# A first room in plain fp32, the smallest room moved to last but one, and a last room that finishes its first tile ahead

## The chip, the cores and the metric

The kernel runs on one NeuronCore of a Trainium2 chip. The metric is the device time of one execution in microseconds (us); the version before was timed in three runs. TensorE (PE in the profile) does matrix products, with its weight loads shown apart as PEld; VectorE (DVE) and ScalarE (ACT) do elementwise work; GpSimd (POOL) prepares indirect transfers; SyncE (SP) issues the plain ones.

## The reference

Attention with a causal window of 128 positions over 8 batches of 576 positions, 8 heads of 64, and then a mixture of experts. A gate keeps the previous token's expert or takes the best one for this token, so a batch's routing is a sequential scan; then each token goes through one of 8 experts (512 to 1024 to 512, with a relu between), scaled by its gate probability.

```python
scores = np.where(mask, scale * q @ k.T + bias, -1e9)          # mask: 0 <= rel < 128
attn = exp(scores - max) / (sum + 1e-09);  x = attn @ v         # x: (8, 576, 512)
for b in range(B):
    for s in range(S):
        fresh_e = argmax(logits[b, s])
        e = fresh_e if s == 0 or local_gate[b, s] < 0.5 else prev_e
        h = np.maximum(x[b, s] @ w1[e], 0.0)
        out[b, s] = p[e] * (h @ w2[e])
```

## The kernel before

**Attention and routing.** The first part works through 32 slots (8 batches, 4 pairs of heads). A recording layer keeps the order of each engine there as it is written, so its instructions all carry the line of one helper, L167; the tables `ORDER` and `LAST` give that order. The tokens of a batch are written to a table in device memory (`xd`). A generator (`tokens`, then `route`) computes the batch's experts step by step between the attention work: PE, ACT and DVE take turns at small operations, each on the result of the one before. The routing of batch 7 can start only when attention is done. It is then advanced by `tick()` calls inside the first visits of the second part, and so are the tables that place the tokens.

**Visits.** The second part is a row of 15 visits (`PLAN`, `visits`, L1200). A visit takes up to 512 rows that one expert has to process, gathers them from `xd` (GpSimd, one indirect transfer for 128 blocks of 128 values, `take`), and multiplies them by that expert's weights. Three visits belong to experts 0, 1 and 2 (256, 384 and 512 rows, the first two known before batch 7 is routed). The other 12 are rooms for the experts by rank of what is left; `ORDER_OF_ROOMS` (L29) sets their order, and their experts are read from a register. In that order the rooms have 512, 288, 384, 416, 256, 288, 384, 192, 256, 384, 224 and 32 rows.

**One visit.** `Fixed.run` (L1021) goes over f = 0..7, eight slices of 128 of the hidden 1024. For each f, PE makes h (four steps kc, N columns), then ACT the relu hh and DVE the rest hl = relu(h) - hh; then `second(f - 1)` adds to one output tile y for each 128 rows. Every product is three matmuls (`three`, L1003 to L1006) of fp32r operands, high times high, high times low and low times high. So the weights and the rows are split in two beforehand. A weight chunk (two slices f of w1 or w2, 512 KB, `wraw`) is cast by ACT (L241) and subtracted by DVE (L243) into `cut`, of which there are six (`SPLITS`), each freed by the visit's last use of the chunk. `wraw` has six buffers too (`RAWS`). The gathered rows (`kr`) are split by `split_x`: per 128 rows a DVE transpose (L188), an ACT cast (L191) and a DVE subtraction (L192) into `qx`; the transposed rows have one buffer, `xtr`. `finish` scales a y by its gate values (ACT or DVE in turn), and `scatter` (L998) writes it to the output rows with an indirect transfer from GpSimd.

**The row of visits.** `Feed` gathers and splits the rows ahead. At each `tick` of a visit it does at most one split step (`turn`) for rows of the next visit and one gather, and every third tick one scatter. After a visit, `Feed.finish` does what is still missing for the next one. The last visit, `Mini` (32 rows), works in plain fp32 with unsplit weights: `first` (L1094) runs inside the visit before, ahead of its last `second`, `turn` transposes, and `Mini.run` (L1108, matmuls at L1084) has no ticks. Where the engines are not pinned to the program's order, the build's scheduler sets it.

## Time and profile before

| what | value |
|---|---|
| median of three runs | 679.7 us (679.34 to 679.98) |
| the profiled execution | 678.48 us, of which the span of the trace is 676.8 us |
| TensorE busy | 656.5 us, 97% of the span |
| DVE, ACT, POOL busy | 466.0, 418.1, 392.6 us |
| HBM traffic | 101.03 MB read, 19.29 MB written |

The profile lists instructions with a start, a duration, engine, line and tiles; an idle stretch ahead of one stands in brackets with what ended it. Durations of PE rows overlap, because matmuls are pipelined: the pace of a series is read from the starts, and a busy share near 100% may hide waits shorter than a matmul. A plain fp32 matmul has two PE rows, an fp32r one has one. In the listing of one visit the three kinds L1004, L1005 and L1006 are the three products of `three`. The execution's time is 1.7 us longer than the span of its trace.

### The profile page before, as it was taken

The page shows a single profiled execution, that of the slowest core. Times are in us where ns is not written, and L with a number is a line of the kernel's source. Part 1 is how long each engine was busy: PE and PEld are TensorE (multiplying, and loading weights), DVE is VectorE, ACT ScalarE, POOL GpSimd, SP SyncE. Part 2 cuts the span into 40 slices and gives each one's busy share as a digit, 9 for nine tenths or more (in the row PEclk, how much of TensorE's full clock was granted, in tenths as well). Part 3 has the DMA queues.
Part 4 walks back from the last instruction along what each step waited for, and adds up shares of the span by engine and source line. Part 5 has one row for each costly group of instructions (what it writes and reads, how often), then busy time and mean ns, then how long its engine had stood idle before and what let it go on. Part 6 is the DMA issues. An engine that isn't in the chain of part 4 may idle for free. (4 is left out here: it accounts for less than half of the span.)

```text
span 676.8 us, 16362 instructions
## 1 busy us (share of the span) xinstructions
PE 656.5 (97%) x5485; PEld 528.0 (78%) x5485; DVE 466.0 (69%) x1637; ACT 418.1 (62%) x1217; POOL 392.6 (58%) x655
## 2 busy tenths in 40 slices
PE   8999999999999989999999999999999999999993
PEld 4667777677666678878888888988898898899882
DVE  6579889889888999975553657453776547774520
ACT  7999999999989644343442555353665536653421
POOL 7856656556687745877775476471577516761011
PEclk9999999999999999999999999999999999999998
DMA  9855754764813675554654268343846834774810
GB/s 287 275 143 156 240 170 144 218 194 152 255 68 110 196 265 179 164 148 148 228 189 135 82 225 281 96 133 128 287 152 205 281 99 143 241 224 152 274 54 34
DMA packets 60903, 121.09 MB, mean 179 GB/s; under 512 B 9260, under 2 KB 28204, under 8 KB 60816
## 3 DMA queue, kind: packets, MB, share of 16 engines
q1 hardware_dynamic: 51248, 100.12, 46.5%
q0 software_dynamic: 9136, 19.30, 9.3%
q8 instruction: 44, 0.72, 0.4%
q10 hardware_dynamic: 432, 0.59, 0.3%
q14 instruction: 43, 0.35, 0.2%
HBM read 101.03 MB, written 19.29 MB: 178 GB/s over the span
## 5 line engine op out<-in xcount | busy, mean ns | idle before, releaser
L182 POOL DMA_INDIRECT kr<-xd,xidx x141 | 155.3, 1101 | 55.3 <-issue 39.4
L1004 PE MATMUL h<-qx,cut 128*128 128x384 f32 (+6 forms) x440 | 142.4, 324 | 0.0
L1005 PE MATMUL h<-qx,cut 128*128 128x384 f32 (+6 forms) x440 | 140.8, 320 | 0.2 <-DVE qx L192 0.2
L1006 PE MATMUL h<-qx,cut 128*128 128x384 f32 (+6 forms) x440 | 140.9, 320 | 0.0
L243 DVE TENSOR_TENSOR cut<-wraw,cut 128x512 fp32r<-128x512 f32 x183 | 118.8, 687 | 30.0 <-ACT cut L241 28.6
L1056 ACT ACTIVATE hh<-h 128x384 fp32r<-128x384 f32 (+4 forms) x104 | 46.6, 448 | 132.9 <-PE h L1006 131.2
L167 POOL TENSOR_SCALAR cut<-cut,r 128x192 f32<-128x192 f32 (+2 forms) x256 | 99.6, 407 | 45.8 <-DVE r L167 16.2
L998 POOL DMA_INDIRECT out<-y,sidx x41 | 44.5, 1085 | 132.7 <-ACT y L1013 85.3
L1057 DVE SCALAR_TENSOR_TENSOR hl<-h,hh 128x256 fp32r<-128x256 f32 (+4 forms) x112 | 55.4, 496 | 88.4 <-ACT hh L1056 88.0
L1004 PE MATMUL y<-cut,hh 128*128 128x512 f32 x288 | 113.7, 395 | 0.8 <-ACT hh L167 0.8
L1006 PE MATMUL y<-cut,hl 128*128 128x512 f32 x288 | 113.1, 394 | 0.9 <-DVE hl L1057 0.9
L1005 PE MATMUL y<-cut,hh 128*128 128x512 f32 x288 | 113.3, 393 | 0.0
L167 ACT ACTIVATE cut<-scs,mn 128x192 f32<-128x192 f32 (+2 forms) x256 | 108.8, 429 | 5.3 <-DVE mn L167 5.0
L241 ACT CAST cut<-wraw 128x512 fp32r<-128x512 f32 x164 | 93.6, 618 | 24.6 <-PE y L1006 23.9
L1004 PEld LDWEIGHTS h<-qx,cut 128*128 128x128 f32 x440 | 83.0, 189 | 9.7 <-issue 3.9
L167 DVE CUSTOM_DVE_ANT_0 scs<-sc,bias 128x192 f32<-128x192 f32 (+2 forms) x288 | 83.1, 324 | 8.9 <-PE sc L167 5.6
L1005 PEld LDWEIGHTS h<-qx,cut 128*128 128x128 f32 x440 | 83.1, 189 | 5.7 <-DVE qx L192 0.7
L1006 PEld LDWEIGHTS h<-qx,cut 128*128 128x128 f32 x440 | 83.2, 189 | 2.7 <-issue 0.2
L167 PE MATMUL pt<-ident,cut 128*128 128x128 f32 x448 | 70.8, 282 | 0.6
L1006 PEld LDWEIGHTS y<-cut,hl 128*128 128x128 f32 x288 | 54.0, 188 | 13.5 <-DVE hl L1057 2.1
L167 PE MATMUL sc<-kr,qx 64*64 64x192 f32 (+2 forms) x1152 | 61.9, 319 | 1.2 <-DVE mn L167 1.2
L1004 PEld LDWEIGHTS y<-cut,hh 128*128 128x128 f32 x288 | 54.2, 188 | 10.7 <-ACT hh L167 1.8
(218 smaller groups left out, 1036.7 us busy)
## 6 DMA issues: line engine op xcount, KB each, us to landing
wraw<-w SPq DMA_DIRECT2D x100, 512.0 KB
xT<-w SPq DMA_DIRECT2D x20, 512.0 KB
kr<-kT SPq DMA_DIRECT2D x31, 288.0 KB
qx<-qT SPq DMA_DIRECT2D x30, 288.0 KB
cut<-v SPq DMA_DIRECT2D x8, 1024.0 KB
xd<-T SPq DMA_DIRECT2D x8, 768.0 KB
xd<-T SPq DMA_DIRECT2D x8, 384.0 KB
kr<-xd,xidx POOLq DMA_INDIRECT x141, 3.8
```

Of the source, the lines that this page charges most:

```text
L167: ins = getattr(self.engine, name)(*args, **kw)
L182: queued(nc.gpsimd.indirect_dma_start(out=r, out_offset=None, in_=src[0:n, :], in_offset=bass.IndirectOffsetOnAxis(ap=col, axis=0), bounds ...
L241: scalar.copy(c[:, 0, f], raw[:, f])
L243: (pool if 2 * n + f == POOL_CUT else vector).tensor_tensor(c[:, 1, f], raw[:, f], c[:, 0, f], ALU.subtract)
L998: queued(nc.gpsimd.indirect_dma_start(out=out.rearrange("t (a c) -> (t a) c", a=n), out_offset=bass.IndirectOffsetOnAxis(ap=col, axis=0), ...
L1004: nc.tensor.matmul(o, ah, bh, start=start, stop=False)
L1005: nc.tensor.matmul(o, ah, bl, start=False, stop=False)
L1006: nc.tensor.matmul(o, al, bh, start=False, stop=stop)
L1056: now.act.activation(hh, hp[:, :M], AF.Relu)
L1057: nc.vector.scalar_tensor_tensor(hl, hp[:, :M], 0.0, hh, ALU.max, ALU.subtract)
```

## The change

Four things are altered.

- The first visit (expert 0, 256 rows) becomes `Plain`: its weights are marked "raw" and used as loaded, its rows are only transposed (`PlainRows`), h and y are plain fp32 matmuls, and there is one relu and no hl. The splitting of its first six chunks and rows is gone from the attention part (`turns`).
- `Stream` counts `wraw` buffers that are held (`live`) where it counted chunks ahead, and lets the splitting go on past chunks that are not split.
- `ORDER_OF_ROOMS` ends 192, 384, 224, 32, 256: the `Mini` room is last but one and the 256-row room of rank 2 is last.
- The last visit runs with `tail`: the scatters of earlier visits are issued ahead of it; the second products of its output tile 1 for f = 5, 6, 7 are kept back; after the last h, tile 0 is completed, finished and scattered, and then tile 1.

```diff
-ORDER_OF_ROOMS = [0, 1, 2, 8, 3, 9, 4, 10, 5, 6, 7, 11]
+ORDER_OF_ROOMS = [0, 1, 2, 8, 3, 9, 4, 10, 6, 7, 11, 5]
...
+    class PlainRows(Rows):
+        def turn(self, t):
+            if self.x is None:
+                self.x = sh.tile([P, self.blocks, KS, 32], F32, name="qx")
+            n = self.last(t)
+            pin(nc.vector.transpose(self.x[:, 4 * t:4 * t + n].rearrange("p b c i -> p (b c i)"), self.r[:, t, :n].rearrange("p q c -> p (q c)")))
...
-            while self.n_raw < len(self.order) and self.n_raw < self.n_cut + RAWS:
+            while self.n_raw < len(self.order) and self.live < RAWS:
...
-            while self.n_cut < len(self.order) and self.n_cut < self.first + self.depth:
+            while self.n_cut <= upto or self.n_cut < min(self.first + self.depth, self.ready):
                 self.load()
-                if self.order[self.n_cut][3] == "only":
+                if self.order[self.n_cut][3] in ("only", "raw"):
...
-        keep = "only" if nb == 1 else "also" if nb % 4 in (1, 2) else None
+        keep = "raw" if kind == "own" and e == 0 else "only" if nb == 1 else "also" if nb % 4 in (1, 2) else None
...
-            yield from W.split(tp.tile([P, 2, 2, DM], F32R, name="xT"), act, dve)
-            for what in (("M4", 4 * NB - 5), ("U3", 4 * NB - 2), ("M4", 4 * NB - 1)):
-                while what not in emitted:
-                    yield
-                yield from W.split(W.room(), act, dve)
...
-                if f > 0:
+                if tail and f == 6:
+                    vh, vl, _ = W.at("b")
+                    hh, hl = hs[5]
+                    three(ys[0], hh[:, 0:P], hl[:, 0:P], vh[:, 1], vl[:, 1], False, False)
+                elif f > 0 and not (tail and f == 7):
                     second(f - 1)
...
+            if tail:
+                assert n == 2 and not rest
+                chunks = [W.at("b"), W.at("b", 1)]
+                for t, fs in ((0, (6, 7)), (1, (5, 6, 7))):
+                    for f in fs:
+                        hh, hl = hs[f]
+                        sl, (vh, vl, _) = slice(P * t, P * t + P), chunks[f // 2 - 2]
+                        three(ys[t], hh[:, sl], hl[:, sl], vh[:, f % 2], vl[:, f % 2], False, f == 7)
+                    c = self.rows.t0 + t
+                    finish(ys[t], self.rows.g[:, t:t + 1], self.rows.idx[2][:, c:c + 1], t)
+                    scatter(*pending.pop())
...
+    class Plain(Fixed):
...
+            def second(f):
+                h, raw = hs.pop(f), W.at("b")
+                for t in range(n):
+                    nc.tensor.matmul(ys[t], h[:, P * t:P * t + P], raw[:, f % 2], start=f == 0, stop=f == 7)
+                    tick()
...
+            for f in range(8):
+                raw = W.at("a")
+                hp = ph_.tile([P, N], F32, name="h")
+                for kc in range(KS):
+                    nc.tensor.matmul(hp, raw[:, f % 2, P * kc:P * kc + P], self.rows.x[:, :, kc], start=kc == 0, stop=kc == KS - 1)
+                hs[f] = mp.tile([P, N], F32, name="hh", bufs=3)
+                now.act.activation(hs[f], hp, AF.Relu)
...
-            mini = visits[i + 1] if i + 2 == len(visits) else None
-            v.run(W, lambda: feed.tick(i + 1), mini, lambda: feed.finish(i + 1))
+            mini = visits[i + 1] if i + 1 < len(visits) and isinstance(visits[i + 1], Mini) else None
+            if i + 1 == len(visits):
+                while pending:
+                    scatter(*pending.pop(0))
+            v.run(W, lambda: feed.tick(i + 1), mini, lambda: feed.finish(i + 1), i + 1 == len(visits))
             feed.finish(i + 1)
```

Lines move by the edit: L1004 to L1006 become L1020 to L1022, L1084 becomes L1118, L241 and L243 become L248 and L250, L1013 becomes L1029, L1011 becomes L1027. L1171 and L1162 are the matmuls of `Plain` for h and y.

PE, where the routing of batch 7 begins inside the first visit (pk are the routing's small tiles). Before:

```order
L1006 MATMUL h_4945<-qx_4410,xT_4708 128x256
L1004 MATMUL y_4894<-cut_4842,hh_4928 128x512
L167 MATMUL pk_4936<-xT_4083,w32_98 32x128 x4
L1005 MATMUL y_4894<-cut_4842,hh_4928 128x512
L167 MATMUL pk_4966<-ident_81,part_4912 128x128 x4
L1006 MATMUL y_4894<-cut_4842,hl_4929 128x512
```

And now, where a row with x4 is four matmuls:

```order
L167 MATMUL pk_4879<-xT_4083,w32_98 32x512 x4
L1171 MATMUL h_4892<-qx_4410,wraw_4085 128x256
L1162 MATMUL y_4868<-wraw_4087,hh_4875 128x512
L167 MATMUL pk_4901<-xT_4083,w32_98 32x128 x4
L1162 MATMUL y_4869<-wraw_4087,hh_4875 128x512
L167 MATMUL pk_4916<-ident_81,part_4878 128x128 x4
L1171 MATMUL h_4928<-qx_4410,wraw_4089 128x256 x4
```

Between two routing steps stand whole plain matmuls now. Ahead of the 32x512 row stand 7 of the 32 h matmuls now, and 19 of the 96 before; behind it stand 25 h and all 16 y matmuls now, and 77 and 48 before.

ACT and then DVE at the end of the 224-row visit and the `Mini` room (hl_9553, hh_9561, y_9645 are the `Mini` room's, y_9580 and y_9582 the 224-row visit's, cut_9640 and qx_9647 the last visit's). Before, ACT ends with the `Mini` room:

```order
L1056 ACTIVATE hh_9940<-h_9927 128x224
L1099 ACTIVATE hl_9967<-h_9950 128x256
L1013 ACTIVATE y_9980<-y_9741,gs_9241 128x512
L1106 COPY hh_9975<-tr_9972 128x256
L1013 ACTIVATE y_10017<-y_9984,gs_9471 128x128
```

Now ACT has:

```order
L1133 ACTIVATE hl_9553<-h_9536 128x256
L1029 ACTIVATE y_9580<-y_9299,gs_8789 128x512
L1140 COPY hh_9561<-tr_9558 128x256
L248 CAST cut_9640<-wraw_9600 128x512 x2
L1029 ACTIVATE y_9645<-y_9584,gs_9021 128x128
L191 CAST qx_9647<-xtr_9648 128x4x128
L191 CAST qx_9647<-xtr_9652 128x4x128
L1072 ACTIVATE hh_9680<-h_9667 128x256
```

And DVE has:

```order
L1027 TENSOR_SCALAR y_9582<-y_9300,gs_8789 128x512
L250 TENSOR_TENSOR cut_9640<-wraw_9600,cut_9640 128x512 x2
L188 STREAM_TRANSPOSE xtr_9648<-kr_9310 128x512
L192 TENSOR_TENSOR qx_9647<-xtr_9648,qx_9647 128x4x128
L188 STREAM_TRANSPOSE xtr_9652<-kr_9310 128x512
L192 TENSOR_TENSOR qx_9647<-xtr_9652,qx_9647 128x4x128
```

The splitting of the last visit's rows stands behind the `Mini` room's work on both engines, after one chunk's splitting; five of its eight chunks are split further up.

PE behind the last h. Before, it ends with the second stage of the `Mini` room:

```order
L1004 MATMUL y_9742<-cut_9824,hh_9940 128x512
L1005 MATMUL y_9742<-cut_9824,hh_9940 128x512
L1006 MATMUL y_9742<-cut_9824,hl_9941 128x512
L1084 MATMUL y_9984<-wraw_9790,hh_9975 32x128 x8
L1084 MATMUL y_9984<-wraw_9829,hh_9975 32x128 x8
L1084 MATMUL y_9984<-wraw_9848,hh_9975 32x128 x8
L1084 MATMUL y_9984<-wraw_9879,hh_9975 32x128 x8
```

Now y_9665 is tile 0 of the last visit and y_9666 tile 1:

```order
L1020 MATMUL y_9665<-cut_9735,hh_9842 128x512
L1021 MATMUL y_9665<-cut_9735,hh_9842 128x512
L1022 MATMUL y_9665<-cut_9735,hl_9843 128x512
L1020 MATMUL y_9666<-cut_9640,hh_9799 128x512
L1021 MATMUL y_9666<-cut_9640,hh_9799 128x512
L1022 MATMUL y_9666<-cut_9640,hl_9800 128x512
L1020 MATMUL y_9666<-cut_9735,hh_9822 128x512
L1021 MATMUL y_9666<-cut_9735,hh_9822 128x512
L1022 MATMUL y_9666<-cut_9735,hl_9823 128x512
L1020 MATMUL y_9666<-cut_9735,hh_9842 128x512
L1021 MATMUL y_9666<-cut_9735,hh_9842 128x512
L1022 MATMUL y_9666<-cut_9735,hl_9843 128x512
```

Nine matmuls of tile 1 stand behind the last one of tile 0, and on GpSimd the two scatters of this visit are the only ones behind them.

## Rows read from the trace of the kernel before

**Rows 1.** Busy time by stretch of the span (us from its start): length, then for each engine busy us and instructions, the granted TensorE clock, DMA share and GB/s.

```profile
200.00:250.00 50.00, 47.38 (x448) 34.98 (x448) 46.59 (x179) 36.88 (x106) 34.62 (x54) 1.00 0.58 185
...
300.00:330.00 30.00, 30.00 (x134) 24.83 (x133) 15.40 (x24) 11.48 (x21) 22.69 (x22) 1.00 0.52 161
...
660.00:677.00 17.00, 5.18 (x100) 3.50 (x92) 0.75 (x1) 1.70 (x4) 2.94 (x3) 0.81 0.10 34
```

**Rows 2.** PE in order of time inside the first visit: start us, us, engine, line, operation. The first row is the routing's first step for batch 7; the last two L1006 rows end the visit and go on with the next one.

```profile
226.56 1.07 PE L167 MATMUL pk<-xT,w 128*32 128x512 f32 x8
...
231.27 0.50 PE L1006 MATMUL y<-cut,hl 128*128 128x512 f32 x1 [0.90 <-DVE hl L1057]
...
233.06 0.33 PE L167 MATMUL pk<-ident,part 128*128 128x128 f32 x1 [0.25 <-DVE L L167]
...
248.09 0.50 PE L1004 MATMUL y<-cut,hh 128*128 128x512 f32 x1 [0.78 <-ACT hh L167]
...
252.16 0.20 PE L167 MATMUL pk<-cw,ro_all 128*128 128x48 f16 x1 [0.62 <-DVE ro_all L167]
...
255.67 0.62 PE L1006 MATMUL y<-cut,hl 128*128 128x512 f32 x2
256.14 0.34 PE L1006 MATMUL h<-qx,cut 128*128 128x384 f32 x1
```

**Rows 3.** PE in order of time, two unbroken series of the first visit: six matmuls of 512 columns with the 256-column series behind them (first and last of each).

```profile
244.33 0.40 PE L1004 MATMUL y<-cut,hh 128*128 128x512 f32 x1
...
245.49 0.39 PE L1006 MATMUL y<-cut,hl 128*128 128x512 f32 x1
245.71 0.28 PE L1004 MATMUL h<-qx,cut 128*128 128x256 f32 x1
...
247.03 0.28 PE L1006 MATMUL h<-qx,cut 128*128 128x256 f32 x1
```

**Rows 4.** PE groups of plain fp32 matmuls, one line for each shape: count, busy us and mean ns. Four of them run beside each other, one in each quarter of the array's columns.

```profile
L167 PE MATMUL pk<-xT,w 128*32 128x512 f32 x8 | 1.1, 604 | 0.0
L1094 PE MATMUL h<-xT,qx 128*32 128x256 f32 x32 | 1.9, 382 | 0.0
```

**Rows 5.** DVE and ACT groups between 216 and 256 us: count, busy us and mean ns.

```profile
L243 DVE TENSOR_TENSOR cut<-wraw,cut 128x512 fp32r<-128x512 f32 x17 | 11.1, 687 | 0.1
...
L1057 DVE SCALAR_TENSOR_TENSOR hl<-h,hh 128x256 fp32r<-128x256 f32 x8 | 3.2, 414 | 0.0
...
L167 ACT CAST cut<-wraw 128x512 fp32r<-128x512 f32 x24 | 13.4, 622 | 0.3 <-PE y L1006 0.3
```

**Rows 6.** All engines at the end of attention, in order of time: a cast of the first visit's weights and one of its rows, a wait of PE for ACT, and between them a subtraction for the weights.

```profile
215.28 0.61 ACT L167 CAST xT<-wraw 128x512 fp32r<-128x512 f32 x1
215.79 0.61 ACT L191 CAST qx<-xtr 128x512 fp32r<-128x512 f32 x1
...
218.63 0.65 DVE L167 TENSOR_TENSOR xT<-wraw,xT 128x512 fp32r<-128x512 f32 x1
...
218.86 0.55 PE L167 MATMUL xb<-pt,cut 128*64 128x128 f32 x8 [0.66 <-ACT pt L167]
```

**Rows 7.** The splitting of 128 rows for a later visit, DVE and ACT in order of time (the third of four tiles of the 512-row visit).

```profile
286.27 0.71 DVE L188 STREAM_TRANSPOSE xtr<-kr 128x512 f32<-128x512 f32 x1
287.01 0.62 ACT L191 CAST qx<-xtr 128x512 fp32r<-128x512 f32 x1 [1.38 <-DVE xtr L188]
287.67 0.69 DVE L192 TENSOR_TENSOR qx<-xtr,qx 128x512 fp32r<-128x512 f32 x1
```

**Rows 8.** All engines but the weight loads at the end of the span, in order of time.

```profile
662.93 0.36 ACT L1106 COPY hh<-tr 128x256 f32<-128x256 f32 x1
663.26 0.75 DVE L1011 TENSOR_SCALAR y<-y,gs 128x512 f32<-128x512 f32 x1 [4.29 <-PE y L1006]
663.31 0.98 POOL L998 DMA_INDIRECT out<-y,sidx  x1 [14.54 <-ACT hh L1106]
663.35 1.96 PE L1084 MATMUL y<-wraw,hh 128*32 128x128 f32 x64
665.37 0.37 ACT L1013 ACTIVATE y<-y,gs 128x128 f32<-128x128 f32 x1 [2.08 <-PE y L1084]
667.23 0.98 POOL L998 DMA_INDIRECT out<-y,sidx  x1 [2.94 <-issue]
670.60 0.98 POOL L998 DMA_INDIRECT out<-y,sidx  x1 [2.39 <-issue]
```

**Rows 9.** The granted clock at the end of the span, in stretches as in the first group; and PE at its start, in order of time, eight and six warming matmuls of 512 columns.

```profile
669.00:670.00 1.00, 0.00 (x0) 0.00 (x0) 0.00 (x0) 0.00 (x0) 0.00 (x0) 1.00 0.28 105
670.00:671.00 1.00, 0.00 (x0) 0.00 (x0) 0.00 (x0) 0.00 (x0) 0.40 (x1) 0.69 0.00 0
...
1.06 3.59 PE L167 MATMUL pk<-warm 128*128 128x512 f16 x8 [1.06 <-DVE warm L167]
9.35 1.47 PE L167 MATMUL pk<-warm 128*128 128x512 f16 x6
```

**Rows 10.** What held up the scatters of L998 over the whole span (us, times), and the time from issue to landing of the weight chunks in `wraw` (us, min/median/max).

```profile
  DMA out<-y,sidx: 8.6, 3
...
DMA to landing us min/median/max: 2.8/3.1/6.5
```

**Rows 11.** The chain of work that ended last, its shares of the span by line.

```profile
by line: issue 0.3%; DMA out<-y,sidx 0.1%; POOL out L998 0.1%; POOLq L1294 0.1%
```

More of the change, by code (lines that the diff above doesn't have):

```diff
@@ L250, in __init__, with paired @@
             self.order = order
-            self.raw, self.cut, self.gone, self.n_raw, self.n_cut, self.first, self.depth = [], {}, set(), 0, 0, 0, 1
+            self.raw, self.cut, self.gone = [], {}, set()
+            self.n_raw = self.n_cut = self.n_room = self.first = self.live = self.ready = 0
+            self.depth = 1
+        def paired(self, i):
+            _, which, _, kind = self.order[i]
+            return kind in ("also", "only") and which == ("b" if kind == "also" else "a")
         def load(self):
-            while self.n_raw < len(self.order) and self.n_raw < self.n_cut + RAWS:
+            while self.n_raw < len(self.order) and self.live < RAWS:
                 e, which, c, kind = self.order[self.n_raw]
-                if kind and which == ("b" if kind == "also" else "a"):
+                if self.paired(self.n_raw):
+                    if self.n_raw > self.first + 2 * SPLITS:
+                        return
                     if c % 2 == 0:
@@ L281, in split, with find, at @@
             self.cut[self.n_cut] = c[:, 0], c[:, 1], raw
+            if not self.paired(self.n_cut):
+                self.live -= 1
             self.n_cut += 1
             yield from split_chunk(raw, c, scalar, vector, self.n_cut - 1 if self is W else 0)
-        def find(self, which):
-            return min(i for i in self.cut if self.order[i][1] == which)
-        def at(self, which):
+        def find(self, which, nth=0):
+            return [i for i in range(self.first, len(self.order)) if self.order[i][1] == which and i not in self.gone][nth]
+        def at(self, which, nth=0):
             self.depth = min(self.depth + 1, SPLITS)
-            self.fill()
-            return self.cut[self.find(which)]
+            i = self.find(which, nth)
+            self.fill(i)
+            return self.cut[i]
         def done(self, which):
@@ L296, in done @@
             self.gone.add(i)
+            if self.order[i][3] in ("only", "raw") and not self.paired(i):
+                self.live -= 1
             while self.first in self.gone:
@@ L803, in turns @@
                 yield
-            while not W.raw or NB - 2 not in read:
-                yield
-            yield from W.split(tp.tile([P, 2, 2, DM], F32R, name="xT"), act, dve)
-            for what in (("M4", 4 * NB - 5), ("U3", 4 * NB - 2), ("M4", 4 * NB - 1)):
-                while what not in emitted:
-                    yield
-                yield from W.split(W.room(), act, dve)
         known, taken, routed, read, emitted = [], [], [], [], []
-        rows0 = [Rows(4 * KS * e, KS * e, 4 * k, idx0, n) for e, (k, n) in enumerate(EARLY)]
+        rows0 = [(Rows if e else PlainRows)(4 * KS * e, KS * e, 4 * k, idx0, n) for e, (k, n) in enumerate(EARLY)]
         side, prep = iter(()), {":": setup(), ";": zeros()}
@@ L1019, in __init__, with run @@
             self.rows = rows
-        def run(self, W, tick, mini=None, ready=None):
+        def run(self, W, tick, mini=None, ready=None, tail=False):
             N = 32 * self.rows.blocks
@@ L1089, in first @@
         def first(self, W):
-            raws = [W.at("a") if i == 0 else W.cut[W.find("a") + i] for i in range(4)]
+            raws = [W.at("a", i) for i in range(4)]
             hp = ph_.tile([P, 256], F32, name="h")
@@ L1093, in first @@
                 for g in range(4):
-                    nc.tensor.matmul(hp[32 * g:32 * g + 32], self.rows.x[:, kc], raws[g][:, :, P * kc:P * kc + P], start=kc == 0, stop=kc == 3,
+                    nc.tensor.matmul(hp[32 * g:32 * g + 32], self.rows.x[:, 0, kc], raws[g][:, :, P * kc:P * kc + P], start=kc == 0, stop=kc == 3,
                                      skip_group_check=True)
@@ L1114, in run @@
             finish(y, self.rows.g[:, 0:1], self.rows.idx[2][:, c:c + 1], 0)
-    class MiniRows(Rows):
-        def turn(self, t):
-            self.x = sh.tile([P, KS, 32], F32, name="qx")
-            pin(nc.vector.transpose(self.x.rearrange("p c i -> p (c i)"), self.r[:, 0, 0]))
+    class Plain(Fixed):
+        def run(self, W, tick, *_):
+            N = 32 * self.rows.blocks
+            n = N // P
+            ys = [py.tile([P, DM], F32, name="y") for _ in range(n)]
+            hs = {}
+            def second(f):
[3 more added lines that the diff above has]
+                    tick()
+                if f % 2:
+                    W.done("b")
+            for f in range(8):
[5 more added lines that the diff above has]
+                now.act.activation(hs[f], hp, AF.Relu)
+                if f % 2:
+                    W.done("a")
+                tick()
+                if f > 0:
+                    second(f - 1)
+                tick()
+            second(7)
+            for t in range(n):
+                c = self.rows.t0 + t
+                finish(ys[t], self.rows.g[:, t:t + 1], self.rows.idx[2][:, c:c + 1], t % 2)
     class Flex:
```

15 lines of the change are left out of this document (10 added, 5 removed).

## Prediction

> **What bounds the kernel now.** I read the table of stretches first [rows 1]. From 300 us on TensorE is busy without a break while DVE and ACT are half idle: there only matmul work counts. Two places are different. In 200 to 250 us TensorE is short of 2.6 us while DVE runs 46.6 of 50: routing, splitting and rows compete there. And the last 17 us hold 5.2 us of TensorE. Then I read TensorE in order of time inside the first visit [rows 2]: its waits end on DVE or ACT operations. Last I read the end [rows 8]: the last matmul ends at 665.31, the last scatter starts at 670.60 and the span ends at 676.8. So the change can pay at the first visit and at the end, and nowhere else.
>
> **First visit, the matmuls.** A series of fp32r matmuls moves on by 0.12 us for 256 columns ((247.03 - 245.71) / 11) and 0.232 us for 512 ((245.49 - 244.33) / 5) [rows 3]. The visit has 96 of the first and 48 of the second: 11.5 + 11.1 = 22.6 us. In plain fp32 the 16 matmuls of L1094 have 32 rows, so eight steps with four side by side: (1.9 - 0.38) / 7 = 0.22 us a step [rows 4], two steps for one full matmul of 256 columns, 0.44 us. For 512 columns I take twice that, 0.88; the two steps of the 32x512 row, (1.07 - 0.60) = 0.47 apart [rows 2, 4], bound it at 0.94. So the visit needs 32 x 0.44 + 16 x 0.88 = 28.2 us: **5.6 us more** matmul work, on the engine that bounds.
>
> **First visit, the waits.** What pays for it are waits. From the routing's first step to the visit's end is 256.14 - 226.56, less two matmuls of the next visit in between (0.35): 29.2 us [rows 2]. In it stood 77 h and 48 y matmuls, 9.2 + 11.1 = 20.3 us. The other 8.9 us are the routing's own matmuls, whose first step takes 1.07 and which I put at 3.5 in all, and waits, 5.4. The four longest waits are 0.90, 0.25, 0.78 and 0.62 [rows 2], 2.55 together; the others are gaps that overlapping durations hide. Each ends with hl, hh or a routing step that stood in DVE's or ACT's queue behind splits. The change takes off those queues 16 of the split halves, 16 x 0.69 = 11 us on DVE and 16 x 0.62 = 10 us on ACT, and eight hl, 3.2 us [rows 5]; one half was given to GpSimd for a later visit and stays. Between two routing steps the order now has 0.9 to 7 us of plain matmuls, and DVE's steps fit under them. Two places stay tight: the scan waits for a hold that stands in ACT's queue behind a cast of the second visit, whose weights are loaded only when a plain chunk is freed and need 3.1 us to land [rows 10]; and ro_all has two chunks and two row tiles of the second visit ahead of it. I leave 0.7 us for both. New length: 25 x 0.44 + 16 x 0.88 + 3.5 + 0.7 = 29.3 us. **So about 0.0** against 29.2; -0.6 if no wait is left, +4.7 if all stay.
>
> **End of attention.** Seven plain h matmuls stand ahead of that first step, 3.1 us, where 19 fp32r ones stood, 2.3 us: +0.8. ACT loses two casts of weights and one of rows there, 0.61 each, DVE subtractions of 0.65 to 0.69, and TensorE's wait of 0.66 for ACT [rows 6] is filled with plain matmuls. The steps that are left wait for each other as before. I take **-0.6**, between -0.9 and +0.8.
>
> **The middle.** The second visit's rows and chunks are split with DVE less loaded. The third visit's rows and the rooms have the same work in another order; TensorE is busy all through [rows 1]. The 192-row room is now followed by 384 rows, which have three tiles to split and not two, 2 us more for ACT and DVE beside 16 us of matmuls, but the room before it has 33 us and six split chunks of reserve. 0.0, up to +1 if that reserve runs out.
>
> **A new wait ahead of the last visit.** `Mini.run` has no ticks, so the last visit's rows are split behind it, and in the order they stand behind the room's work. DVE: y from 663.26 to 664.01 [rows 8], two halves of a chunk at 0.69 less overlap to 665.3 [rows 5]. Then, for each of two tiles, transpose, cast, subtraction: casts start 0.74 after the transpose, subtractions 0.66 after that, and end 0.69 later [rows 7], 2.0 to 2.1 a tile with one `xtr` between them. The second ends at 665.3 + 4.1 = 669.4. The `Mini` matmuls end at 663.35 + 1.96 = 665.31 [rows 8]. Until 669.4 TensorE has two matmuls that need only high parts, 0.24. **+3.9 us**, on the path, with nothing to hide it: before, all other visits' rows were split under the visit ahead. Bounds 3.3, if the one late chunk is split sooner, and 4.7, if its 3.1 us load is late [rows 10].
>
> That idle time touches the clock. The rows show the granted clock at 1.00 until past 670 us, with the last matmul ended at 665.31 [rows 8, 9]; a wait of 3.9 us, with two matmuls in it, is shorter than those 5 us, so I add nothing. The Trainium skill, "TensorE: Matmul & The Clock Gate", section "Why this matters for your kernels", advises against idle gaps between bursts of matmuls, since after one the engine is back at half its clock. By that rule the sum would be 682.0, the clock rival's time below; no row here shows a fall inside the kernel.
>
> **The end.** Before, three scatters were left when the last visits ended; each waits for the one before to land (8.6 us in three such waits [rows 10]), so they start 3.92 and 3.37 us apart, the last one 670.60 - 665.31 = 5.3 us behind the last matmul [rows 8]. Now the older ones go out under the last visit's 22.6 us. Tile 0 is complete nine matmuls ahead of the end, 9 x 0.232 = 2.1 us. Its scaling and the start of its scatter take about 1.1 us (0.75 and two hand-overs), so the first scatter starts 1.0 us before the last matmul ends, and the second 3.4 to 3.9 later: 2.4 to 2.9 behind it. **-2.6 us** (-2.9 to -2.0, a last transfer of 256 KB being longer than the `Mini` one).
>
> **Sum.** 0.0 - 0.6 + 0.0 + 3.9 - 2.6 = +0.7. The profiled execution took 678.48 (span 676.8, 1.7 around it) and would take 679.2. It lies 1.2 below the median of the runs, 679.7, to which I add the same 0.7: **680.4**. A measurement of this kernel can tell about 0.2% from no change, 1.36 us; the sum lies inside.
>
> **Rivals.**
> - *The routing is a chain of latencies, not a queue behind splits* (slower). Then the waits that are named stay and only the hidden gaps go: 2.7 us left where I took 0.7, 682.4. For it: the 0.62 wait ends with a routing step, not with a split. Against it: DVE was over 90% busy there. From 1.4 us of waits left on, the verdict is slower. Chance 0.20.
> - *The clock falls in the new wait* (slower). At the span's start eight warming matmuls took 3.59 us and six took 1.47 later [rows 9]; eight at the later pace take 1.96, so one such spell costs 1.6: 682.0. Against it are the 5 us of rows 9. Chance 0.10.
> - *The first tile ahead doesn't do what it says*: the end is set by something behind the scatters, and nothing comes off, 683.0. For it: 6.2 us lie between the last scatter's start and the end of the span. Against it: the chain that ended last runs through the scatters [rows 11]. Chance 0.05.
> - *The waits go altogether* (faster): none is left in the first visit (-0.7), attention ends 0.9 earlier (-0.3), the row split starts as soon as it may (-0.6), the tail gives 2.9 (-0.3), and the third visit's short wait for its rows goes (-0.5): 680.4 - 2.4 = 678.0. Chance 0.14.
>
> **How the numbers follow.** The forecast has 0.45, the four rivals 0.49, and 0.06 is for sums in between, half each in same and slower. Faster is the last rival, 0.14; same is the forecast with its share, 0.48; slower is 0.20 + 0.10 + 0.05 and its share, 0.38. The range goes from 678.2, near the faster rival, to 683.2, past the slower ones; it leaves out a clock fall together with routing waits, and the best sums.
>
> **What would show it.** In the changed profile: L1171 rows 0.22 us apart and L1162 rows 0.44, two to a matmul; no named wait over 0.5 us between the routing's first step and the second visit, which come 29.3 us apart; an idle stretch ahead of the last visit's first L1021 of some 4 us that ends on DVE qx L192; two L1014 scatters 3.4 to 3.9 us apart at the end, the second 2.4 to 2.9 behind the last matmul; the granted clock 1.00 in the last visit. The prediction is wrong if the first visit keeps its waits, if the rows of the last visit are split under the `Mini` room after all, or if the granted clock falls there.

## The result and the profile after

The changed kernel takes **687.7 us** (median of 4 runs, 686.23 to 690.20) beside 679.6 for the kernel before (679.34 to 679.98): ratio 1.0122, 95% interval 1.0088 to 1.0156. It is slower by 8.0 us where 0.7 was forecast. The profiled execution took 688.69 (span 686.9), 10.2 more than that of before, so the sum below is made against 10.1 us of span; two of the four runs have a mean granted clock of 0.989 (688.7 and 690.2 us), two of 0.993 (686.2 and 686.7). Ten of the later runs were made on two chips on which the kernel before itself takes 760 to 783 us; of those only the order of events and ratios within one chip are read.

TensorE, which was never short of work behind 300 us, now has holes. The stretches, as in [rows 1]:

```profile
200.00:250.00 50.00, 48.02 (x397) 31.20 (x397) 31.67 (x145) 27.63 (x87) 33.69 (x55) 0.97 0.46 142
...
550.00:600.00 50.00, 48.23 (x287) 40.76 (x286) 31.26 (x56) 26.56 (x60) 23.18 (x21) 1.00 0.46 141
...
640.00:660.00 20.00, 15.71 (x152) 12.49 (x151) 9.92 (x18) 8.32 (x17) 3.00 (x3) 0.83 0.42 132
```

DVE has 31.7 us in 200 to 250 where it had 46.6, as intended. But 1.8 us of PE are missing in 550 to 600 and 4.3 in 640 to 660, and the granted clock is below 1.00 in two stretches. PE's waits from 240 us on by what ended them (us in total, times, longest):

```profile
PE h L1020 <- ACT qx L191: 3.9, 1, 3.9
PE y L1020 <- ACT hh L1072: 1.7, 1, 1.7
PE pk L167 <- DVE hr L167: 1.4, 1, 1.4
PE h L1021 <- DVE qx L192: 0.6, 1, 0.6
PE tr L1138 <- ACT hl L1133: 0.4, 1, 0.4
```

Three of them count; in order of time they are the third, the second and the first row. The last row stands in the `Mini` room and fits that room's 0.4 in the sum below. **In the first visit**, all engines in order of time:

```profile
240.90 1.14 ACT L167 CAST cut<-wraw 128x512 fp32r<-128x512 f32 x2 [4.37 <-DMA wraw<-w]
241.55 1.29 DVE L250 TENSOR_TENSOR cut<-wraw,cut 128x512 fp32r<-128x512 f32 x2 [7.58 <-ACT cut L167]
...
241.94 0.58 ACT L167 ACTIVATE hold<-pk 1x512 f32<-1x512 f32 x1
...
242.76 1.20 DVE L167 TENSOR_TENSOR_SCAN hr<-hold,pk 1x512 f16<-1x512 f32 x1
...
244.01 0.19 PE L167 MATMUL pk<-identb,rcb 128*1 128x64 f16 x1 [1.43 <-DVE hr L167]
```

ACT and DVE are not busy here, they are blocked: ACT stood idle 4.37 us for a chunk of the second visit to land, and `hold`, a 0.58 us step that the scan `hr` needs, stands behind that chunk's casts. Behind the wait the granted clock is down, from 245.6 to 249.0 us:

```profile
244.00:246.00 2.00, 1.99 (x11) 1.25 (x11) 1.48 (x5) 0.76 (x2) 0.00 (x0) 0.89 0.85 273
246.00:248.00 2.00, 2.00 (x9) 0.84 (x8) 1.76 (x4) 1.25 (x4) 0.00 (x0) 0.50 1.03 414
248.00:250.00 2.00, 2.00 (x7) 1.14 (x6) 1.97 (x9) 1.40 (x4) 1.28 (x1) 0.76 0.29 109
```

The shares lost, (0.11 + 0.50 + 0.24) x 2 us, make 1.7 us by which these matmuls took longer; that the visit lost less by them is shown further down. **In the 192-row room**, all engines in order of time:

```profile
568.95 0.69 DVE L192 TENSOR_TENSOR qx<-xtr,qx 128x512 fp32r<-128x512 f32 x1 [0.69 <-ACT qx L191]
...
569.68 0.71 DVE L188 STREAM_TRANSPOSE xtr<-kr 128x512 f32<-128x512 f32 x1
...
570.42 0.62 ACT L191 CAST qx<-xtr 128x512 fp32r<-128x512 f32 x1 [1.50 <-DVE xtr L188]
570.95 0.27 ACT L1072 ACTIVATE hh<-h 128x128 fp32r<-128x128 f32 x1
...
571.27 0.50 PE L1020 MATMUL y<-cut,hh 128*128 128x512 f32 x1 [1.73 <-ACT hh L1072]
```

`hh` takes 0.27 us and its matmuls are long done, but ACT waits 1.50 us ahead of it with the cast of the next visit's third row tile, whose transpose waits for the one `xtr` buffer. **Ahead of the last visit** PE and ACT in order of time, and the granted clock by stretch:

```profile
642.00 1.93 PE L1128 MATMUL h<-xT,qx 128*32 128x256 f32 x32
...
646.29 1.96 PE L1118 MATMUL y<-wraw,hh 128*32 128x128 f32 x64
...
651.47 0.62 ACT L191 CAST qx<-xtr 128x512 fp32r<-128x512 f32 x1 [1.50 <-DVE xtr L188]
...
652.14 0.79 PE L1020 MATMUL h<-qx,cut 128*128 128x256 f32 x2 [3.89 <-ACT qx L191]
...
653.25 0.41 PE L1022 MATMUL h<-qx,cut 128*128 128x256 f32 x1
...
655.17 0.41 PE L1022 MATMUL h<-qx,cut 128*128 128x256 f32 x1
...
659.75 0.28 PE L1022 MATMUL h<-qx,cut 128*128 128x256 f32 x1
...
660.83 0.28 PE L1022 MATMUL h<-qx,cut 128*128 128x256 f32 x1
```

```profile
648.00:652.00 4.00, 0.25 (x12) 0.00 (x0) 2.72 (x5) 1.52 (x3) 0.00 (x0) 0.97 0.71 247
652.00:659.00 7.00, 6.86 (x28) 6.40 (x29) 1.59 (x4) 1.45 (x5) 1.98 (x2) 0.53 0.09 34
659.00:678.00 19.00, 19.00 (x117) 16.55 (x116) 5.00 (x10) 4.58 (x10) 0.98 (x1) 1.00 0.01 4
```

The pitch of a 256-column matmul is 0.213 us ((655.17 - 653.25) / 9) until about 658.5 and 0.12 afterwards. PE was idle from 648.25 (646.29 + 1.96) to 652.14, and the clock fell to 1.2 GHz at 651.7. **The end**, all engines in order of time, beside [rows 8]:

```profile
675.99 0.69 ACT L1029 ACTIVATE y<-y,gs 128x512 f32<-128x512 f32 x1 [1.06 <-PE y L1022]
...
676.96 0.98 POOL L1014 DMA_INDIRECT out<-y,sidx  x1 [18.53 <-ACTq L1362]
...
677.63 0.39 PE L1022 MATMUL y<-cut,hl 128*128 128x512 f32 x1
678.05 0.75 DVE L1027 TENSOR_SCALAR y<-y,gs 128x512 f32<-128x512 f32 x1 [2.66 <-PE y L1022]
680.44 0.98 POOL L1014 DMA_INDIRECT out<-y,sidx  x1 [2.51 <-issue]
```

The terms of the sum, from the starts of the visits in both traces:

| step | forecast | measured | from |
|---|---|---|---|
| end of attention | -0.6 | -0.2 | `pk<-xT` at 226.36 and 226.56 |
| first visit, to the third visit's first matmul | 0.0 | +3.3 | 296.40 - 226.36 and 293.33 - 226.56 |
| the middle | 0.0 | +2.2 | 192-row room 23.69 and 21.56; a 384-row room 33.51 and 33.43 |
| `Mini` room | none | +0.4 | 642.00 to 648.25, 659.48 to 665.31 |
| new wait | +3.9 | +3.9 | 648.25 to 652.14 |
| clock in the last visit | 0 | +3.2 | 652.14 to 678.02 = 25.88; a 256-row room of before 22.64 |
| end | -2.6 | -2.6 | 686.9 - 678.02 and 676.8 - 665.31 |
| sum | +0.7 | +10.2 | |

### The profile page after: what moved, and what is told of

Its sections match the earlier page's. It is cut to its first block, busy times and chain, and to the rows that moved or that the text cites. A ratio compares the mean times of both kernels' runs of the same rounds, so it can differ in the third digit from the quotient of the medians.

```text
span 686.9 us, 16221 instructions
## 1 busy us (share of the span) xinstructions
PE 665.2 (97%) x5437; PEld 527.7 (77%) x5437; DVE 453.5 (66%) x1612; ACT 409.0 (60%) x1199; POOL 389.3 (57%) x655
## 5 line engine op out<-in xcount | busy, mean ns | idle before, releaser
L250 DVE TENSOR_TENSOR cut<-wraw,cut 128x512 fp32r<-128x512 f32 x175 | 113.4, 687 | 43.2 <-ACT cut L248 34.5
L1020 PE MATMUL h<-qx,cut 128*128 128x384 f32 (+6 forms) x416 | 136.4, 329 | 3.9 <-ACT qx L191 3.9
L1021 PE MATMUL h<-qx,cut 128*128 128x384 f32 (+6 forms) x416 | 135.2, 325 | 0.7 <-DVE qx L192 0.6
L1022 PE MATMUL h<-qx,cut 128*128 128x384 f32 (+6 forms) x416 | 135.5, 326 | 0.0
L1072 ACT ACTIVATE hh<-h 128x384 fp32r<-128x384 f32 (+4 forms) x104 | 46.6, 448 | 136.1 <-PE h L1022 133.3
L1073 DVE SCALAR_TENSOR_TENSOR hl<-h,hh 128x384 fp32r<-128x384 f32 (+4 forms) x104 | 52.2, 502 | 93.5 <-ACT hh L1072 93.4
L248 ACT CAST cut<-wraw 128x512 fp32r<-128x512 f32 x164 | 93.4, 618 | 31.1 <-PE y L1022 21.4
L1020 PE MATMUL y<-cut,hh 128*128 128x512 f32 x272 | 107.4, 395 | 1.7 <-ACT hh L1072 1.7
L1022 PE MATMUL y<-cut,hl 128*128 128x512 f32 x272 | 107.0, 394 | 0.0
L1021 PE MATMUL y<-cut,hh 128*128 128x512 f32 x272 | 107.0, 393 | 0.0
L1020 PEld LDWEIGHTS h<-qx,cut 128*128 128x128 f32 x416 | 79.4, 191 | 14.0 <-ACT qx L191 4.5
L1021 PEld LDWEIGHTS h<-qx,cut 128*128 128x128 f32 x416 | 79.6, 191 | 6.4 <-DVE qx L192 1.7
L1022 PEld LDWEIGHTS h<-qx,cut 128*128 128x128 f32 x416 | 79.7, 192 | 2.8 <-issue 0.2
L167 PEld LDWEIGHTS pt<-ident,cut 128*128 128x128 f32 x448 | 49.3, 141 | 15.7 <-ACT cut L167 4.2
L1022 PEld LDWEIGHTS y<-cut,hl 128*128 128x128 f32 x272 | 51.2, 188 | 12.0 <-DVE hl L1073 1.1
```

The lines of the kernel that those rows point to most:

```text
L167: ins = getattr(self.engine, name)(*args, **kw)
L248: scalar.copy(c[:, 0, f], raw[:, f])
L250: (pool if 2 * n + f == POOL_CUT else vector).tensor_tensor(c[:, 1, f], raw[:, f], c[:, 0, f], ALU.subtract)
L1020: nc.tensor.matmul(o, ah, bh, start=start, stop=False)
L1021: nc.tensor.matmul(o, ah, bl, start=False, stop=False)
L1022: nc.tensor.matmul(o, al, bh, start=False, stop=stop)
```

## The experiments

Theory: three waits, each for a step that stands behind something else in the order of ACT or DVE, cost the time, and the clock falls behind them; neither the plain matmuls nor the first tile ahead does. Rival: the plain matmuls are too dear. Second rival: the clock falls for what ran, not for the idle time. All diffs are against the changed kernel, and `...` stands where lines are left out.

**One part each.** `e4_plain_only` is the kernel before with the plain visit alone, `e5_no_plain` the changed kernel without it, `e6_no_tail` without the first tile ahead:

```diff
 e4, e6:
-            if i + 1 == len(visits):
-                while pending:
-                    scatter(*pending.pop(0))
-            v.run(W, lambda: feed.tick(i + 1), mini, lambda: feed.finish(i + 1), i + 1 == len(visits))
+            v.run(W, lambda: feed.tick(i + 1), mini, lambda: feed.finish(i + 1))
 e4:
-ORDER_OF_ROOMS = [0, 1, 2, 8, 3, 9, 4, 10, 6, 7, 11, 5]
+ORDER_OF_ROOMS = [0, 1, 2, 8, 3, 9, 4, 10, 5, 6, 7, 11]
 e5:
...
-        rows0 = [(Rows if e else PlainRows)(4 * KS * e, KS * e, 4 * k, idx0, n) for e, (k, n) in enumerate(EARLY)]
+        rows0 = [Rows(4 * KS * e, KS * e, 4 * k, idx0, n) for e, (k, n) in enumerate(EARLY)]
...
-            visits.append((Fixed if e else Plain)(rows0[e] if e < len(EARLY) else Rows(0, 0, nb, idxs)))
+            visits.append(Fixed(rows0[e] if e < len(EARLY) else Rows(0, 0, nb, idxs)))
```

> The kernel before with the plain fp32 first visit alone (old order of rooms, no first tile ahead). Theory: the first visit and its surroundings cost 3.1 us, a wait of 1.4 us for the scan and a stretch at half clock behind it (1.6 us) among them: 679.6 + 3.1 = 682.7, and nothing else changes. Rival, the plain matmuls are the main cost of the whole change (5.6 us more matmul work that no wait pays for): 685 to 688.

> The changed kernel with the first visit as it was before (split weights and rows, fp32r), but the new order of rooms and the last visit's first tile ahead. Theory: the wait ahead of the last visit (3.9), the half clock behind it (3.2), a wait in the 192-row room (2.1), 0.4 in the Mini room, less 2.6 at the end, are all there without the plain visit: 679.6 + 7.0 = 686.6. Rival, the plain matmuls are the main cost: 680 to 681.

> The changed kernel without the last visit's first tile ahead (its two tiles finish in step again, scatters not flushed ahead of it); plain first visit and order of rooms kept. Theory: the tail gave 2.6 us, so 687.7 + 2.6 = 690.3, with two scatters some 3.5 us apart whose second starts 4 to 5.5 us behind the last matmul. Rival, with one visit less at the end the order alone gave the gain: 687.7 to 688.2.

Beside 679.1 for the kernel before, the plain visit alone took 681.7 (ratio 1.0038, 1.0025 to 1.0052), the rest without it 685.5 (1.0096, 1.0081 to 1.0111), and without the first tile ahead 692.0 (1.0185, 1.0171 to 1.0199). Theory had 682.7, 686.6 and 690.3. The first two add up to 8.9, beside 8.0 for the whole change: the plain visit is the smaller part, and the rival that puts the loss on its matmuls falls. The new way of `Stream` stands in all three and was not tried alone; in `e5`, with it and without the plain visit, it is 67.5 us from the routing's first step to the third visit, and 66.8 before. From the last matmul to the end of the span it is 11.05 us without the tail and 8.88 with it, so the tail is worth 2.2 us by the traces. The medians of `e6` and the changed kernel are 4.3 apart; in the trace of `e6` the clock also fell in the 192-row room, where it did not in the changed kernel's.

**The new wait and the clock.** `e1_rows_early` splits the last visit's rows under the 224-row room; `c4_filler` leaves them late and keeps TensorE busy.

```diff
 e1 (new lines alone):
...
+                self.x = sh.tile([P, self.blocks, KS, 32], F32, **({"name": "qx"} if self.blocks > 1 else {"name": "qm", "bufs": 1}))
...
+            v.run(W, lambda: feed.tick(i + 2 if mini else i + 1), mini, lambda: feed.finish(i + 1), i + 1 == len(visits))
 c4:
+                ah = W.at("a")[0]
+                hp = ph_.tile([P, DM], F32, name="h")
+                for _ in range(16):
+                    nc.tensor.matmul(hp, ah[:, 0, :P], ah[:, 0], start=True, stop=True)
```

> The changed kernel with one thing moved: the last visit's two row tiles are split during the 224-row room instead of behind the Mini room (the Mini room's rows get a tile of their own so that a buffer is free). Theory: the idle stretch ahead of the last visit (3.9 us) goes, and with it the stretch at half clock that follows it (25.9 us for the last visit instead of 22.6, so 3.2 us): 687.7 - 7.1 = 680.6, granted clock 1.00 from 640 us to the last matmul. Rival, the clock falls for another reason than the idle stretch (the Mini room's own matmuls of 32 rows, or the history of the run): only the 3.9 us go, 683.8, and a stretch at 0.50 stays in the last visit.

> The changed kernel with 16 extra matmuls of 512 columns (3.7 us, their result is read by nobody) put into the idle stretch ahead of the last visit; the rows are split as late as before. Theory: the idle stretch is what brings the clock down; with TensorE busy there the granted clock stays 1.00, the last visit takes 22.6 us instead of 25.9, and the time is 687.7 - 3.2 = 684.5. Rival, the clock falls for what ran before (the Mini room's 32-row matmuls): a stretch at 0.50 stays and the time is 687.7 or more.

`e1` took 683.2 (1.0061, 1.0047 to 1.0075). Its profiled execution (span 680.1) is 6.8 shorter than that of the changed kernel, 6.6 of it behind the start of the `Mini` room, where 7.1 was expected. The medians differ by 4.4 only, nearer the rival's 3.9 than the 7.1. The traced execution is the fastest of the five, with a mean clock of 0.997 beside 0.990 to 0.995; falls of the clock behind the waits that are left (below) would fit, but there is no trace of the others. The stretches of `e1` and then of `c4` from 648 us on:

```profile
648.00:655.00 7.00, 7.00 (x68) 6.37 (x57) 3.32 (x7) 2.67 (x7) 1.00 (x1) 1.00 0.50 178
655.00:671.00 16.00, 16.00 (x99) 13.98 (x97) 3.50 (x8) 3.76 (x8) 1.90 (x2) 1.00 0.02 5
```

```profile
648.00:655.00 7.00, 6.74 (x84) 4.92 (x83) 4.76 (x7) 2.96 (x6) 1.58 (x2) 1.00 0.57 191
655.00:678.00 23.00, 22.62 (x142) 20.05 (x142) 6.23 (x13) 5.93 (x13) 2.79 (x3) 1.00 0.04 12
```

In both the clock stays at 1.00. In `c4` the rows are as late as in the changed kernel (10.08 us from the `Mini` room's start to the last visit's, 10.14 there), and the last visit takes 23.36 us instead of 25.88. Of the ten traces of the other chips, the three with that idle stretch (changed kernel, `e5`, `e6`) have a fall there, and the five whose last visit follows the `Mini` room without it (`e1`, `c4`, and `c1` to `c3` below) have none: the idle stretch brings the clock down, not the `Mini` room's matmuls. The time of `c4` shows nothing of it: 687.4 (1.0127, 1.0111 to 1.0144). In its trace the wait in the 192-row room was followed by a fall, which made that room 3.1 us longer (26.80). Of its other four executions there is no trace; three have a higher mean clock (0.994 to 0.995) than the changed kernel ever had and yet 686.8 to 687.4 us. That stays open.

**The room's wait and the scan's.** `c1_rows_swap` (with `e1`'s edit) puts the 192-row room ahead of the 224-row one, `c2_rows_swap_lag` also splits a chunk one release later in the first visit, `c3_rows_swap_noplain` is `c1` with `e5`'s edit, without the plain visit.

```diff
 c1, c2, c3:
+ORDER_OF_ROOMS = [0, 1, 2, 8, 3, 9, 4, 6, 10, 7, 11, 5]
 c2:
...
-            self.ready = self.n_raw
+            self.ready, self.seen = self.seen if self.first < 8 else self.n_raw, self.n_raw
```

> The run with the last visit's rows split early, and the 192-row room put behind the second of the two 384-row rooms, so that under it the two row tiles of the 224-row room are split and not three of a 384-row room. Theory: the wait of 1.7 us in the 192-row room came from ACT's queue, where hh stood behind casts of a third row tile; it goes, the room takes 21.6 us again instead of 23.7: 683.2 - 2.1 = 681.1. Rival, the room is short of split weights: the wait stays or moves to the next visit, 683.2.

> As the run with rows early and rooms swapped, and in the first visit a chunk of the second visit is split only two releases behind its load and not one, so that hold stands ahead of that chunk's casts in ACT's queue, and the scan ahead of its subtractions in DVE's. Theory: hold stood behind casts whose weights had not landed; the wait of 1.5 us for the scan goes, and with it the stretch at half clock that follows it in some executions (1.6 us): 681.1 - 1.5 to 3.0 = 678.1 to 679.6. Rival, the routing is a chain of latencies: the wait moves to its next step or to the second visit's rows, 680.5 to 681.1.

> As the run with rows early and rooms swapped, with the first visit as in the kernel before (split weights and rows, fp32r). Theory: the order of rooms then costs only some 0.6 us in the Mini room and the first tile ahead gives 2.5: 679.1 - 1.9 = 677.2, faster than both kernels. Rival, the gain at the end is used up by the work that the order moved into the last visits: 679 to 680.

683.3, 683.3 and 682.4 us (1.0067, 1.0055 and 1.0046): nothing won over `e1`, and all three sums missed (681.1, 678.1 to 679.6, 677.2); `c1` has the time of its rival, a wait that moves to the next visit. With two row tiles to split, the 192-row room took 21.4 us in all three, so the third tile was its cause. But the next room now waits 1.8 to 3.0 us. ACT in `c1`, in order of time:

```profile
632.45 1.14 ACT L248 CAST cut<-wraw 128x512 fp32r<-128x512 f32 x2 [4.96 <-DMA wraw<-w]
633.50 0.61 ACT L191 CAST qx<-xtr 128x512 fp32r<-128x512 f32 x1
634.01 0.35 ACT L1072 ACTIVATE hh<-h 128x224 fp32r<-128x224 f32 x1
```

Again `hh` behind casts of a chunk that has not landed. That weights come late there because the `Mini` room keeps four unsplit chunks in the six `wraw` buffers is argued from the code, not shown. ACT in `c2`, in order of time:

```profile
235.88 0.57 ACT L167 ACTIVATE hold<-pk 1x512 f32<-1x512 f32 x1
241.25 1.14 ACT L167 CAST cut<-wraw 128x512 fp32r<-128x512 f32 x2 [4.80 <-DMA wraw<-w]
242.29 0.38 ACT L167 ACTIVATE hh<-h 128x256 f32<-128x256 f32 x1
242.57 0.20 ACT L167 ACTIVATE hold<-pk 1x64 f32<-1x64 f32 x1
```

The first `hold` is free at 235.88, six us earlier, and the second now stands behind the same landing: the wait (1.49 us) moved by one step. It ended at 243.49, 17.67 us behind the routing's first step, where the changed kernel has 17.65. So it is the landing, not the routing's own chain, that sets this wait.

**An attempt at all three waits.** `f1_rows_order` is `e1` with one of the 256-row rooms behind the 192-row room, as before the change; `f2_defer_one` and `d3_defer_more` also hold back the second visit's splitting in the first visit; `g1_defer_one` is `f2` again, `f4_filler_clean` is `f2` with late rows and the filler, `g2_rows_order_noplain` is `f1` with `e5`'s edit.

```diff
 f1 and the others:
+ORDER_OF_ROOMS = [0, 1, 2, 8, 9, 4, 10, 3, 6, 7, 11, 5]
 f2, g1, f4 (d3 with 4 for 3):
-            while self.n_cut <= upto or self.n_cut < min(self.first + self.depth, self.ready):
+            while self.n_cut <= upto or self.n_cut < min(self.first + self.depth, self.ready, 8 + max(0, self.first - 3) if self is W and self.first < 8 else 999):
```

> The run with rows early and the new order of rooms once more, on a chip where the kernel before takes its usual time. Theory A (three row tiles held up hh in the 192-row room): the wait of 1.7 us there is gone and comes back nowhere: 683.2 - 2.1 = 681.1. Theory B (the visits ahead of the Mini room run short of weights): a wait of 1.7 us or more in the 256, 384 or 224-row rooms, 683.

> As the run before it, and in the first visit the second visit's chunks are split from its fourth release on, one per release. Theory: what the scan waited for was the landing of a chunk whose casts stood ahead of hold in ACT's queue; the wait of 1.5 us goes, and the stretch at half clock that follows it in some executions: 681.1 - 1.5 to 3.0 = 678.1 to 679.6. Rival, the scan is bound by the routing's own steps: the wait stays, 681.

> As the run before it, with the chunks of the second visit split from the fifth release on. Theory: no wait for the scan either, but the second visit's first chunk now comes late, or its casts are in the way of the table's last steps: 0 to 1 us more than from the fourth release. Rival: both waits gone, the same as from the fourth release or less.

> New order of rooms and late splitting in the first visit, so that no other wait is left to bring the clock down; the last visit's rows are split behind the Mini room as in the changed kernel, and 16 extra matmuls (3.7 us, read by nobody) fill the stretch. Theory: the rows cost their 3.9 us and the clock nothing: the time of the run with late splitting plus 3.9, 682 to 683.5, last visit 23.4 us at granted clock 1.00. Rival: the clock falls with a busy engine too, plus 7, 685 to 687.

> Rows of the last visit split early, new order of rooms, and the second visit's chunks split from the first visit's fourth release on, one per release. Theory: all three of the change's waits are gone (hr at most 0.3 us, no hh wait in the 192-row room, no idle stretch ahead of the last visit), the granted clock stays at 1.00, and the time is 678.1 to 679.6: the plain visit pays for itself and the end's 2.5 us are nearly all that is left. Rival: the visits ahead of the Mini room run short of weights (a wait of 1.7 us or more in the 256, 384 or 224-row rooms) or the routing keeps its wait: 681 to 683.

> Rows early and the new order of rooms, with the first visit as in the kernel before. Theory: 0.9 us lost in the Mini room and 2.5 us won at the end against the kernel before: 679.1 - 1.6 = 677.5. Rival, weights run short ahead of the Mini room: 679 to 681.

These and four further runs of the same kernels (`d1_rows_order` as `f1`, `d2_defer_one` as `f2`, `d4_rows_order_noplain` and `f3_rows_order_noplain` as `g2`) were made on the two chips named above; their times decide nothing. The ratios are 1.0016 (0.9942 to 1.0090) for `f1` and 1.0012 for `d1`; 1.0126, 1.0017 and 0.9999 for `f2`, `d2` and `g1`; 0.9967 for `d3`; 1.0125 for `f4`; 0.9952, 0.9906 and 0.9952 for `f3`, `d4` and `g2`, which are one kernel. The interval of `d4` (0.9833 to 0.9979) lies below 1 and that of `f2` (1.0052 to 1.0200) above it, but those of the same two kernels run again (`f3`, `g2`; `d2`, `g1`) have 1 inside. On these chips all of PE, DVE and ACT are short of work together at many places, for example in `f1`, where the stretch has 10.00 us of PE in the changed kernel:

```profile
300.00:310.00 10.00, 3.16 (x16) 2.20 (x15) 2.54 (x9) 2.03 (x4) 7.62 (x8) 0.84 0.28 80
```

The rooms can't be read there, the first visit can. ACT in `f1` and then in `f2`, in order of time:

```profile
257.72 1.14 ACT L167 CAST cut<-wraw 128x512 fp32r<-128x512 f32 x2 [4.03 <-DMA wraw<-w]
258.76 0.58 ACT L167 ACTIVATE hold<-pk 1x512 f32<-1x512 f32 x1
...
261.06 0.21 ACT L167 ACTIVATE hold<-pk 1x64 f32<-1x64 f32 x1 [1.46 <-PE pk L167]
```

```profile
253.56 0.57 ACT L167 ACTIVATE hold<-pk 1x512 f32<-1x512 f32 x1
257.63 0.38 ACT L167 ACTIVATE hh<-h 128x256 f32<-128x256 f32 x1 [3.50 <-PE h L1171]
257.92 0.20 ACT L167 ACTIVATE hold<-pk 1x64 f32<-1x64 f32 x1
```

With no cast ahead of either `hold`, the profile names no wait of PE for `hr` in any of the five runs that hold back (`f2`, `d2`, `g1`, `d3`, `f4`), and waits of 1.1 and 1.6 us in `f1` and `d1`. From the routing's `pk<-ident,part` on PE to the table step `tz<-pk` on DVE it is:

| first visit | us |
|---|---|
| as before (before, `c3`, `e5`) | 22.7, 22.7, 23.3 |
| plain (after, `e1`, `e4`, `e6`, `c1`, `c2`, `c4`) | 26.2, 25.9, 26.4, 25.9, 26.1, 26.8, 26.0 |
| as before, on the two chips (`d4`, `f3`, `g2`) | 23.3, 23.3, 22.0 |
| plain, on the two chips (`f1`, `d1`) | 27.0, 28.8 |
| plain and held back, on the two chips (`f2`, `d2`, `g1`, `d3`, `f4`) | 24.7, 23.9, 23.5, 23.8, 25.2 |

## Why the prediction was wrong

*What held.* The plain matmuls cost what was said. PE in the first visit, in order of time:

```profile
249.10 1.89 PE L1171 MATMUL h<-qx,wraw 128*128 128x256 f32 x8
250.82 1.88 PE L1162 MATMUL y<-wraw,hh 128*128 128x512 f32 x4
252.54 1.89 PE L1171 MATMUL h<-qx,wraw 128*128 128x256 f32 x8
```

By the starts, eight steps of 256 columns take 1.72 us, 0.215 a step and 0.43 a matmul, and four steps of 512 columns take 1.72, 0.86 a matmul. The new wait is 3.9 and ends on `qx`, split behind the `Mini` room's work as worked out. The end gave 2.6: two scatters 3.48 us apart, the second 2.4 behind the last matmul.

*The clock step failed: the sum put it at nothing, and it cost 3.2.* The sum added nothing, because [rows 9] showed 1.00 for 5 us after the last matmul. That was read as a time that every wait has to itself. Here the clock fell 3.5 us after the `Mini` room's last matmul. Nor is 5 us the rule at the end of the span: from the last matmul to the fall there it is 5.1 us in the kernel before, the longest of the ten traces, and between 1.9 (`c1`) and 4.5 in the others. The rival was the right mechanism at half its price: eight warming matmuls gave 1.6, while the spell lasted 6.4 us with PE busy and cost 3.2 by the 256-row room of before, 2.5 by `c4`. The Trainium skill, "TensorE: Matmul & The Clock Gate", section "Why this matters for your kernels", warned of such gaps; the runs agree with it for this wait of 3.9 us.

*The first visit: the place was named, its size was not, and it is the other large term (+3.3).* The scan behind casts of a chunk that lands late and `ro_all` were the two tight places, with 0.7 us for both. In this trace the first took 1.43, `ro_all` has no wait, the second visit's rows behind it have one of 0.63, and the matmuls at half clock took 1.7 longer: 3.1 over what was left. But the fall of the clock is not what the visit lost. From the end of the scan's wait to the second visit's first matmul, in the changed kernel and then in `e1`, where no fall followed:

```profile
244.01:256.20 12.19, 12.19 (x49) 7.02 (x49) 10.74 (x37) 5.20 (x12) 1.28 (x1) 0.86 0.72 239
244.27:256.27 12.00, 11.59 (x49) 6.49 (x49) 10.80 (x38) 4.98 (x12) 1.30 (x1) 1.00 0.72 235
```

With the fall it is 12.19 and 12.18 us (after, `e4`), without it 11.94 to 12.03 (`e1`, `e6`, `c1`, `c4`): the fall cost 0.2. At full clock PE stood idle for 0.4 us of that time instead, and its small matmuls on `ro_all` took 0.87 us beside 0.26. From the routing's first step to the third visit's first matmul it is 66.8 to 67.5 us without the plain visit (before, `c3`, `e5`) and 69.6 to 70.8 with it, fall or not. So the step that failed is the term of 0.7 us for what would be left of the visit's 5.4 us of waits: some 4 us were left (0.7 + 3.3). DVE is still busy for 10.8 of those 12 us; what of the 3.3 is due to that, and what to the late start behind the landing, stays open. The rival with 2.7 us of waits comes near the size, but its cause is not shown: `c2` and `f2` show for the scan that it was held up by what the program put ahead of it in ACT's queue, and not by the routing's step before. Less work on ACT and DVE didn't help ahead of the scan, since both stood blocked with 4.37 and 7.58 us idle.

*The middle: the wrong condition was looked at.* The bound of +1 was tied to the reserve of split chunks. The 2.1 us came from ACT's order instead: three row tiles through one `xtr`, ahead of `hh`, in a room whose `h` takes 1.3 us.

*The end of attention* gave 0.2, not 0.6, by the two traces. One execution of each kernel doesn't tell these apart: in the ten traces the routing's first step starts at 225.5 to 226.6 us with the plain visit and at 226.6 to 227.1 without it, so 0.6 fits as well.

The range left out a clock fall together with routing waits, and that is what came, with the wait in the 192-row room on top.

No version was shown to beat the kernel before. The first tile ahead is worth 2.2 to 2.6 us, but moving the `Mini` room forward to get it brought the waits in the 192-row room and ahead of the last visit, which are there without the plain visit too (`e5`). Whether early rows with the order of `f1` keep the gain stays open, as does the full price of the plain visit without its wait: by the middle values of the table's rows for the two chips, held back and as before, 0.6 us (23.9 and 23.3), of that stretch alone.

## What to carry to other kernels

Work that is taken off an engine pays only if the step that is waited for moves forward in that engine's queue: look at what stands ahead of it there, above all for something that waits for a DMA or for a single buffer. A new wait on TensorE is to be priced with the half clock behind it. It cost up to 3.2 us here where TensorE had no other wait ahead (last visit; 3.1 in the 192-row room of `c4`), and 0.2 in the first visit, where it would have waited anyway. It came behind all five waits of 2.8 us and more, and behind four of fourteen of 1.4 to 1.8. When a visit moves forward, follow what is prepared under it and which buffers it holds, not its own matmuls alone.

## What the runs showed that was not expected

A short wait of TensorE is a gamble. The waits of over 1.4 us in the traces of the ten kernels that ran on the other chips (the kernel before has none behind 200 us), and whether a stretch at 0.50 followed:

| wait of PE, us | followed by a fall | not followed |
|---|---|---|
| 1.42 to 1.84 | 1.43 (after), 1.59 (`e4`), 1.73 (`e6`), 1.73 (`c4`) | 1.73 (after), 1.52, 1.73 (`e1`), 1.42, 1.73 (`e5`), 1.53 (`e6`), 1.84, 1.83 (`c1`), 1.49 (`c2`), 1.66 (`c4`) |
| 2.81 to 4.08 | 2.81 (`c2`), 3.00 (`c3`), 3.53 (`e5`), 3.89 (after), 4.08 (`e6`) | none |

The same wait of 1.73 us, in the same room, was followed by a fall in two kernels and not in three. The stretches at 0.50 last 3.4 us (six of the nine, as after, 245.6 to 249.0) or 6.8 (three, as after, 651.7 to 658.6), so one fall lengthens the matmuls in it by 1.7 to 3.4 us, less what of it is idle. That would explain why the changed kernel's runs spread over 4 us and those of before over 0.6; one traced execution says little of a median here. The Trainium skill, "TensorE: Matmul & The Clock Gate", section "Part 1: The HAM clock gate", says of the clock's rise at a kernel's start that its moment varies between runs of one kernel; for the fall behind a wait the table shows no fixed moment either.
